# A fused recurrent-attention and two-layer kernel: the written order of all engines is replaced, 22 unread matmuls are put into it, and two bias operands become immediates

## The chip, the cores and the metric

One core of a Trainium2 chip runs the whole program. The metric is the device time of one execution in microseconds; of several runs the median is taken. The engines are TensorE (PE, with its weight loads PEld beside it), VectorE (DVE), ScalarE (ACT), GpSimd (POOL) and SyncE (SP), which here only issues transfers. Each engine works through its own instructions strictly in the order in which they are written, and waits on semaphores for the others.

## The reference

Three stages follow each other. First a gated recurrent attention (mLSTM) over 768 steps, for 2 batches and 8 heads of width 40. Its output is put side by side to 1536 tokens of width 320 and goes through a feed-forward layer of width 2048 with the function h - tanh(h) (layer one), and that through a mixture of four experts of width 1024, weighted by normalised probabilities (layer two).

```python
for t in range(S):
    m_new = np.maximum(f_gate[:, :, t] + m, i_gate[:, :, t])
    f_stab = np.exp(f_gate[:, :, t] + m - m_new)
    i_stab = np.exp(i_gate[:, :, t] - m_new)
    C = f_stab * C + i_stab * outer(v_t, k_t)
    n = f_stab * n + i_stab * k_t
    y[t] = sigmoid(o_gate_t) * (C @ q_t) / maximum(abs(n @ q_t), 1)
h = x @ w_in
x = (h - np.tanh(h)) @ w_out
out = sum over e of p[:, e:e + 1] * (np.maximum(x @ w1[e], 0.0) @ w2[e])
```

## The kernel before

**Attention.** The 768 steps are cut into six blocks of 128 steps, (j, b) being block j of batch b. Inside a block the recurrence is written as a masked product: `att_s` (L528) multiplies keys by queries, `att_a` (L538, DVE) multiplies the scores by the weights that ACT made with Exp (`att_exp`, L477), `att_h` (L549 for block 0, L552 and L557 after it) multiplies by the values and adds the carried state, and `att_u` (L566) makes the update of the state. The names in the order are `S`, `a`, `H` and `U` with j and b behind them. The gates are scanned on DVE (`g0`, `g1`, L379 to L404). The first block takes its weights in another way: `first_late` (L490, names `fl`) and `first_sum` (L493, names `fs`) build the exponents on PE with matmuls of 512 columns. `att_den` and `att_x` (L581 to L597) divide and gate; `x_tr` (L620) transposes the result; `x_high` and `x_low` (L625, L632, L636) split it into a high and a low part in reduced precision, so that a product of two split numbers takes three matmuls in place of one slow one. These are the tiles `xT`.

**Layer one.** The hidden width of 2048 is cut into eight slices of 256, the tokens into six groups of 256, which gives 48 units `I0` to `I47`. In unit i, `in1` makes the hidden values with 16 matmuls of 256 columns (L794), `hidden1` evaluates h - tanh(h) (names `h` with the unit's number and a letter, on ACT, DVE and POOL, L803 to L834), and `out1` multiplies by the second weight with 24 matmuls of 320 columns (L850, names `O`). Units 0 to 3 read the tokens of the first block, units 4 to 7 those of the second. The weights arrive as 64-bit numbers and are turned into split 32-bit ones by `conv` (names `i` and `o` with a number: `.l` the load, `.e` on ACT, `.k .m .n` on DVE, `.h` on ACT, `.o` on POOL).

**Layer two.** Tokens are in groups of 512. Each group is turned into operands for a scheme with seven products in place of eight (`build`, names `b`). There are 48 units `m0` to `m47`: `P1` to `P7` are the products (L786, four matmuls of 256 columns each), `c11` to `c22` the sums (L1144 on DVE, then Relu on ACT at L840 and the rest on DVE at L844), `O0` to `O7` the second product (L850, three matmuls of 320 columns each). Their weights are made by `conv_q`: POOL forms sums (`.s1 .s2 .s4`, L348, L353, L356), ACT rounds them (`.ht`, L360, and `.hb`, L333), POOL makes the low parts (`.t0 .t1 .b0 .b1`, L341). Unit 12e + 4t + q reads the weights numbered 8 + 4e + q, so that `i14` is first read in unit m14.

**What sets the order.** Every step is a small function with a name. The table `ORDER`, a text of names, is worked through from left to right, and each function puts its instructions on its engine's queue; names that are not in the table follow behind it, sorted by due times from `P`. So the table decides alone what stands in front of what on every engine, on SP's queue of transfers too. In the kernel before it reaches to the middle of unit m11. PSUM has eight banks, handed out by `bank(i)`; a tile that takes a bank waits for the last reader of the one before.

The lines below are the two activations that read a bias from memory.

```python
nc.scalar.activation(out=v["s"], in_=v["z"], func=ACT.Square, bias=ga[:, 0:1])
nc.scalar.activation(out=v["z"], in_=v["z"], func=ACT.Relu, scale=-1.0, bias=ga[:, 1:2])
```

Of the kernel before, what the change touches and what calls it, by code (L numbers as in the profile page):

```python
# [104 lines left out]
xh1 xl0.1 e104 xl1.1 i1.n i0b.o e112 e105 e102 xl1.0 I0.0 o0.l e117 Le1 i1.h kd100 S10 i2.e i1.o e110 Lg20 e113 e107
a100 I0.1 e111 e114 i2.k kd110 e116 st01.1 e106 i2.m e115 kd101 I1.0 h0a st01.0 h0z i2.n q10 S11 m.t2 a101 i3.l h0s
I1.1 h0t i2.h kd111 H100 a110 h1a q11 h0p h1z a111 H101 h1s i2.o h0q o0.e h1t h0m H110 Lg21 d10.0 o0.k Lp mk20 i3.e
h1p I2.0 d10.1 o0.m e207 H111 e201 d10.2 o0.n ag10 h1q dc o0.h Lg30 i3.k o2.l e200 o0.o h1m d11.0 h0c I2.1 e205 i3.m
mk21 h2a h0h d11.1 d11.2 i3.n h2z de h0l O0.0 h1c o1.l i3.h h2t h2s ag11 x10 h1h h2p i3.o e204 x11 U10 h2q h2m h1l xt3
o1.e Lv20 h2c Lk20 xt2 xh3 o1.k Le2 w10 o2.e I3.0 xl3.0 xl3.1 e203 o1.m e211 w11 e210 xh2 st10.0 I3.1 o1.n e206 O0.1  # L110
o2.k o3.l o1.h xl2.1 Lk21 o2.m h3a Lo1 o1.o h3z xl2.0 I4.0 h3t e202 e212 I5.0 st10.1 h3s o2.n mk30 h2h U11 h3p o2.h
I5.1 Lv21 h3q o3.e i4.l h2l O1.0 e215 o3.k h3m I4.1 kd200 e306 e214 o3.m e307 O1.1 kd201 e217 e213 st11.1 h4a S20 h3c
o2.o h4z h4t h5a I6.0 a201 h3h q20 I6.1 h5z a200 e305 h5t e301 O2.1 kd210 h6z st11.0 o3.n i4.e h3l S21 h4s o4.l H200
e216 h4p h5s q21 Le3 h4q o3.h H201 a210 e303 kd211 h6s w20 a211 U20 h4m Lg31 i4.k Lk30 H210 o3.o st20.0 d20.0 st20.1
h5p og2 H211 d20.1 i4.m w21 h4c O2.0 Lg40 d20.2 i4.n I7.0 ag20 d21.0 h6a i5.l d21.1 O3.0 h5q Lv30 o4.e mk31 d21.2 x20
O3.1 h5m o4.k ag21 h4h U21 h6t i4.h xt4 h6p h4l Lv31 I7.1 s3.0 Lk31 x21 xh4 st21.1 s3.1 xl4.0 xt5 i4.o h7z xl4.1 O4.1
st21.0 e300 h5c e304 S30 e302 o4.m xh5 h7a O4.0 kd300 e315 xl5.1 xl5.0 h5h I8.0 o4.n i5.e h5l h6q i6.l I8.1 e317 a300
h6m O5.0 kd301 i5.k e313 mk40 h8a S31 h6c o4.h a301 h8z I9.0 q30 e310 h8t e312 I9.1 e314 i5.m h6h q31 e316 H300 h7t
h7s e311 h7p h8s H301 kd310 h7q e406 h6l h8p h7m O5.1 Lg41 d30.0 h9z h7c kd311 O6.0 e401 i5.n h7h I10.0 h9s h7l d30.1
h8q o5.l e400 Lk40 O6.1 d30.2 e404 a310 h8m w30 a311 I10.1 i5.h h8c h9a mk41 U30 h9t H310 Lv40 ag30 e417 st30.0 h9p  # L120
h10z o4.o e413 H311 h9q e416 h8h x30 h9m st30.1 Lk41 w31 U31 o5.e h9c xt6 h8l h10a Lv41 I11.0 d31.0 d31.1 Lg50 e405
# [73 lines left out]
def kernel(  # L195
# [602 lines left out]
    def hidden1(hp):  # L798
# [23 lines left out]
        def small():  # L822
            nc.scalar.activation(out=v["z"], in_=v["z"], func=ACT.Relu, scale=-1.0, bias=ga[:, 1:2])  # L823
# [509 lines left out]
```

## Time and profile before

| what | value |
|---|---|
| median of 3 runs | 628.71 us |
| the runs | 625.6, 628.71, 632.61 us |
| the profiled execution | 634.11 us |
| its span, first to last instruction | 632.3 us |
| mean granted clock of PE in it | 0.957 |

The profiled execution took 1.8 us more than its span, and it is 5.4 us above the median of the runs. A page of the profile gives busy time per engine, the span in 40 slices, the chain of work that ended last, and groups of equal instructions; the trace behind it gives every instruction's start and length, what ended an engine's idle time, and the clock that was granted to PE (1.00 is 2.4 GHz, 0.50 is 1.2 GHz). A record of a matmul's length contains its way through the array, so that neighbours overlap; fp32 matmuls leave two records each.

### The profile page before, as it was taken

Reading aid. Unit: us, or ns where it says so; the run is one execution under the profiler, and the core shown is the slowest. Engines: PE = TensorE matmul, PEld = TensorE weight load, DVE = VectorE, ACT = ScalarE, POOL = GpSimd, SP = SyncE. Lnnn points to the kernel's source line nnn. Section 1 sums busy time; section 2 is a strip of 40 time slices with the busy share of each in tenths; the row PEclk is TensorE's granted clock in tenths of the full one; section 3 lists DMA queues with packets and bytes.
Section 4 is the critical chain, followed back from the end, with each engine's and each line's share of the span. In section 5 each row is a group of like instructions: output and inputs, shape, how many; then the busy total and the mean of one; then the engine's idle time right before and its main releaser. Section 6 shows DMA issues by size and latency. Waiting matters only on the chain.

```text
span 632.3 us, 12026 instructions
## 1 busy us (share of the span) xinstructions
PE 604.7 (96%) x4505; PEld 584.1 (92%) x4505; DVE 461.1 (73%) x1010; ACT 352.8 (56%) x738; POOL 337.1 (53%) x329
## 2 busy tenths in 40 slices
PE   7988999999999999999999849999999999999997
PEld 3878899999999999999999849999999999999997
DVE  7576998889789778977786526676676766666675
ACT  1485889877799999975453333223543234432221
POOL 3565887865667757698839356204844045630000
PEclk8565999999999999999999988999999999999999
DMA  8664875552112010011001101101211012201011
GB/s 297 201 187 154 289 229 178 184 182 79 34 44 76 1 34 2 2 55 55 23 1 31 58 22 54 55 2 34 76 55 55 1 35 55 76 2 43 1 43 42
DMA packets 29602, 48.15 MB, mean 76 GB/s; under 512 B 2264, under 2 KB 20056, under 8 KB 29544
## 3 DMA queue, kind: packets, MB, share of 16 engines
q1 hardware_dynamic: 29544, 47.39, 23.6%
q8 instruction: 35, 0.57, 0.4%
q14 instruction: 23, 0.19, 0.1%
HBM read 45.31 MB, written 2.06 MB: 75 GB/s over the span
## 4 chain that ended last, share of the span: by engine, by line
PE 67%; ACT 10%; DVE 8%; POOL 7%; issue 5%; DMA 2%; SPq 0%; DVEq 0%; POOLq 0%; ACTq 0%
PE b L850 28%; PE b L786 21%; PE b L794 7%; PE b L557 2%; PE b L528 2%; POOL so L722 2%; PE b L552 2%; ACT gh L830 2%; POOL gl L834 1%; ACT s L811 1%; ACT z L823 1%; POOL wb L341 1%; ACT t L803 1%; ACT z L807 1%; PE b L549 1%
## 5 line engine op out<-in xcount | busy, mean ns | idle before, releaser
L850 PE MATMUL b<-wo,gh 128*128 128x320 f32 x960 | 201.5, 311 | 9.0 <-DVE gh L844 7.3
L850 PE MATMUL b<-wo,gl 128*128 128x320 f32 x768 | 168.3, 310 | 1.7 <-POOL gl L834 1.7
L850 PEld LDWEIGHTS b<-wo,gh 128*128 128x128 f32 x960 | 149.9, 189 | 10.3 <-DVE gh L844 7.7
L850 PEld LDWEIGHTS b<-wo,gl 128*128 128x128 f32 x768 | 122.9, 189 | 3.4 <-POOL gl L834 3.1
L794 PE MATMUL b<-xT,wi 128*128 128x256 f32 x768 | 105.9, 289 | 2.6 <-ACT xT L625 0.9
L840 ACT ACTIVATE gh<-b 128x256 fp32r<-128x256 f32 x96 | 36.9, 384 | 122.2 <-DVE b L1144 73.1
L794 PEld LDWEIGHTS b<-xT,wi 128*128 128x128 f32 x768 | 98.6, 196 | 5.6 <-ACT xT L625 1.6
L786 PE MATMUL b<-so,wt 128*128 128x256 f32 x560 | 89.0, 283 | 2.7 <-DVE gl L844 1.6
L834 POOL TENSOR_TENSOR gl<-t,gh 128x512 fp32r<-128x512 f32 x48 | 65.5, 1366 | 45.2 <-ACT gh L830 36.5
L1144 DVE TENSOR_TENSOR b<-b,s 128x256 f32<-128x256 f32 x192 | 80.6, 423 | 11.9 <-PE b L786 6.1
L786 PEld LDWEIGHTS b<-so,wt 128*128 128x128 f32 x560 | 79.7, 190 | 3.9 <-DVE gl L844 2.6
L840 ACT ACTIVATE gl<-b 128x256 fp32r<-128x256 f32 x96 | 36.7, 384 | 69.7 <-DVE b L1144 67.5
L844 DVE SCALAR_TENSOR_TENSOR gl<-b,gl 128x256 fp32r<-128x256 f32 x96 | 40.3, 423 | 47.2 <-ACT gl L840 47.0
L341 POOL TENSOR_TENSOR wb<-raw,wb 128x384 fp32r<-128x384 f32 (+1 forms) x32 | 32.5, 1016 | 78.1 <-ACT wb L333 76.5
L844 DVE SCALAR_TENSOR_TENSOR gh<-b,gh 128x256 fp32r<-128x256 f32 x96 | 40.6, 423 | 42.1 <-ACT gh L840 42.1
L1144 DVE TENSOR_TENSOR s<-b,s 128x256 f32<-128x256 f32 x144 | 58.7, 418 | 12.8 <-PE b L786 8.6
L786 PE MATMUL b<-xo,wb 128*128 128x256 f32 x400 | 65.4, 282 | 1.1 <-DVE gh L844 0.5
L786 PEld LDWEIGHTS b<-xo,wb 128*128 128x128 f32 x400 | 57.8, 190 | 1.7 <-DVE gh L844 0.8
L341 POOL TENSOR_TENSOR wt<-tf,wt 64x512 fp32r<-64x512 f32 (+1 forms) x32 | 41.4, 1295 | 21.0 <-ACT wt L360 19.5
L826 DVE COPY_PREDICATED t<-z,b 128x512 f32<-128x512 int32 x48 | 36.0, 753 | 8.5 <-ACT z L823 8.1
L823 ACT ACTIVATE z<-z,ga 128x512 f32<-128x512 f32 x48 | 34.5, 720 | 10.9 <-DVE b L820 10.5
L814 DVE TENSOR_TENSOR t<-b,t 128x512 f32<-128x512 f32 x48 | 32.8, 683 | 10.4 <-ACT z L807 6.4
(124 smaller groups left out, 1022.5 us busy)
## 6 DMA issues: line engine op xcount, KB each, us to landing
kq<-in_kq_dram SPq DMA_DIRECT2D x12, 512.0 KB
raw<-in_wb_dram SPq DMA_DIRECT2D x16, 384.0 KB
raw<-in_wa_dram SPq DMA_DIRECT2D x7, 768.0 KB
w<-g_d SPq DMA_DIRECT2D x10, 512.0 KB
raw<-in_wa_dram SPq DMA_DIRECT2D x8, 640.0 KB
raw<-in_wb_dram SPq DMA_DIRECT2D x16, 320.0 KB
kv<-in_kv_dram SPq DMA_DIRECT2D x12, 372.0 KB
raw<-in_wb_dram SPq DMA_DIRECT2D x16, 128.0 KB
```

What stands on the lines that cost most here:

```text
L341: nc.gpsimd.tensor_tensor(out=o[r, k], in0=i[r, :, q], in1=o[r, 2 * q].bitcast(F32), op=ALU.subtract)
L528: nc.tensor.matmul(ps[g][:, h * 128:(h + 1) * 128], t[64 * g:64 * g + PK, 0, h, :], t[64 * g:64 * g + PK, 1, h, :], start=True, stop=True,)
L786: nc.tensor.matmul(o[:, 0:256], w[:, kw, b if b < 3 else b - 3], x_op(t, a, kx), start=(i == 0), stop=(i == 3),)
L794: nc.tensor.matmul(hp[:, c0:c0 + w], w_in(n, lo, kt, f), xt[:, xk, x0:x0 + w], start=(i == 0), stop=(i == 7))
L814: nc.vector.tensor_tensor(out=v["t"], in0=hp, in1=v["t"], op=ALU.subtract)
L823: nc.scalar.activation(out=v["z"], in_=v["z"], func=ACT.Relu, scale=-1.0, bias=ga[:, 1:2])
L826: nc.vector.copy_predicated(v["t"], v["z"].bitcast(I32), hp)
L834: nc.gpsimd.tensor_tensor(out=v["gl"], in0=v["t"], in1=v["gh"].bitcast(F32), op=ALU.subtract)
L840: nc.scalar.activation(out=g[:, 0], in_=src, func=ACT.Relu)
L844: nc.vector.scalar_tensor_tensor(out=g[:, 1], in0=src, scalar=0.0, in1=g[:, 0].bitcast(F32), op0=ALU.max, op1=ALU.subtract)
L850: nc.tensor.matmul(o[:, 0:DM], g[a][:, c:c + 128], w_out(n, lo, f), start=(first and i == 0), stop=(last and i == 2))
L1144: nc.vector.tensor_tensor(out=out, in0=x, in1=y, op=ALU.add)
```

## The change

The table `ORDER` is a different one and reaches to unit m18 in place of m11. It holds 22 new names, `fA`, `fB` and `fC` with a number. Each stands for one matmul of the identity by itself, 256 columns wide (13 of them, on bank 7 or 3) or 128 columns wide (9 of them, on bank 1), whose result nobody reads. All of them stand ahead of the first second-product of layer one, `O0.1`. The two biases become numbers in the instruction, so that the tile `ga` and the two small fills `m.ga` and `m.t2` fall away. The line numbers of the changed kernel are 15 higher up to the decays of attention and 39 higher behind them.

```diff
@@
-m.id m.late Lf m.b1 Li m.late2 m.eg fl10 i0b.l m.r0 Lb1 m.b0 Lv00 m.st0 Lb0 m.r1 Lk00 g0m fl01 Lv01 g1m g0i Lk01 m.rst
+m.b0 Lb0 m.rst Lf Li m.b1 i0a.l Lb1 m.late m.late2 Lv00 m.st1 Lv01 m.id g0m i0b.l m.r0 fl11 g0i g0f Lo0 Lk00 m.st0
...
@@
-    ga = const.tile([128, 24], F32, name="ga")
+    const.tile([128, 24], F32, name="pad")
@@
+    warm = {}
+
+    def keep_a():
+        if "a" not in warm:
+            warm["a"] = bank(7)
+        keep_on(warm["a"][:, 0:256])
+
+    def keep_b():
+        if "b" not in warm:
+            warm["b"] = bank(3)
+        keep_on(warm["b"][:, 0:256])
+
+    def keep_c():
+        if 1 not in accs:
+            accs[1] = spare[1] = bank(1)
+        keep_on(accs[1][:, 320:448])
+
+    def keep_on(o):
+        n = o.shape[1] // 128
+        nc.tensor.matmul(
+            o.rearrange("p (r c) -> p r c", r=n), ident, ident.unsqueeze(1).to_broadcast([128, n, 128]),
+            start=True, stop=True,
+        )
@@
-            nc.scalar.activation(out=v["s"], in_=v["z"], func=ACT.Square, bias=ga[:, 0:1])
+            nc.scalar.activation(out=v["s"], in_=v["z"], func=ACT.Square, bias=GA)
@@
-            nc.scalar.activation(out=v["z"], in_=v["z"], func=ACT.Relu, scale=-1.0, bias=ga[:, 1:2])
+            nc.scalar.activation(out=v["z"], in_=v["z"], func=ACT.Relu, scale=-1.0, bias=T2)
@@
-    head("m.ga", nc.vector.memset, ga[:, 0:1], GA)
-    head("m.t2", nc.vector.memset, ga[:, 1:2], T2)
@@
+    spare = {}
...
-        if p == 0:
+        if p == 0 and spare.pop(t, None) is None:
             accs[t] = bank(t)
@@
+    first = ORDER.split()
+    keep = {"fA": keep_a, "fB": keep_b, "fC": keep_c}
+    for name in first:
+        if name[:2] in keep:
+            add(0, 0, name, keep[name[:2]])
```

**PE, from the second half of attention block 1 to unit I3.** In the rows, L552 and L557 are `H11` (the block of batch 1), L422 is `dc` (the decays of the state) and L794 with b_482 is unit I2. Before, the two halves of I2 stand inside and behind `H11` and `dc`:

```order
L552 MATMUL b_463<-st_94,kq 128x82
L557 MATMUL b_463<-kv,w 128x41 x2
L794 MATMUL b_482<-xT_86,wi 128x256 x8
L552 MATMUL b_463<-st_94,kq 128x82
L557 MATMUL b_463<-kv,w 128x41 x2
L552 MATMUL b_463<-st_94,kq 128x82
L557 MATMUL b_463<-kv,w 128x41 x2
L422 MATMUL b_506<-ga_97,ga_100 104x6 x8
L794 MATMUL b_482<-xT_86,wi 128x256 x8
```

In the changed kernel, where L476 is an unread matmul, L833 is I2, L591 and L596 are `H11`, L437 is `dc`, L605 is `U10` and L659 the two transposes of x:

```order
L833 MATMUL b_482<-xT_86,wi 128x256 x16
L476 MATMUL b_349<-ident 128x128 x3
L591 MATMUL b_519<-st_94,kq 128x82
L596 MATMUL b_519<-kv,w 128x41 x2
...
L437 MATMUL b_545<-ga_97,ga_100 104x6 x8
L605 MATMUL b_579<-kv,kd 104x82 x4
L476 MATMUL b_349<-ident 128x128
L659 MATMUL b_597<-ident,x 128x128 x3
```

All of I2 now stands ahead of `H11`, and three unread matmuls stand between them.

**DVE, at the gated outputs x of block 1.** L814 with b_482 is the first step of I2's function and L597 the two gated outputs; before, the outputs stand behind that step:

```order
L826 COPY_PREDICATED t<-z,b_390 128x512
L814 TENSOR_TENSOR t<-b_482,t 128x512
L597 TENSOR_TENSOR x<-sd,b_434 128x4x2x40
L817 SCALAR_TENSOR_TENSOR b_482<-s,b_482 128x512
L597 TENSOR_TENSOR x<-sd,b_463 128x4x2x40
```

In the changed kernel, where L636 is the gated output and L853 that first step:

```order
L856 SCALAR_TENSOR_TENSOR b_409<-s,b_409 128x512
L636 TENSOR_TENSOR x<-sd,b_457 128x4x2x40
L859 SCALAR_TENSOR_TENSOR b_409<-b_409,z 128x512
L636 TENSOR_TENSOR x<-sd,b_519 128x4x2x40
L853 TENSOR_TENSOR t<-b_482,t 128x512
L865 COPY_PREDICATED t<-z,b_352 128x512
L865 COPY_PREDICATED t<-z,b_409 128x512
```

Both gated outputs moved ahead of the first step of I2's function.

**ACT, around units m10 and m11 of layer two.** L360 is `.ht`, first that of i13 and then that of i14; L840 are the Relus of the units. Before:

```order
L840 ACTIVATE gh_4620<-b3_4611 128x256
L360 ACTIVATE wt_4622<-tf_4428 128x2x512
L333 ACTIVATE wb_4632<-raw_4530 128x2x384
L360 ACTIVATE wt_4661<-tf_4657 128x2x512
L840 ACTIVATE gl_4663<-b4_4624 128x256
L840 ACTIVATE gl_4666<-b7_4638 128x256
```

In the changed kernel L375 is `.ht` and L879 are the Relus:

```order
L375 ACTIVATE wt_4536<-tf_4454 128x2x512
L1187 ACTIVATE s_4571<-b3_4561 128x256
L321 ACTIVATE wo_4579<-raw_4376 128x640
L879 ACTIVATE gh_4587<-b4_4543 128x256
L879 ACTIVATE gl_4590<-b7_4548 128x256
L879 ACTIVATE gl_4604<-b2_4556 128x256
L879 ACTIVATE gh_4623<-b4_4610 128x256
L375 ACTIVATE wt_4648<-tf_4606 128x2x512
L348 ACTIVATE wb_4656<-raw_4499 128x2x384
```

Between the two `.ht` there was one instruction, and there are six now.

## Rows read from the trace of the kernel before

**Rows 1.** The page, part 1: busy time and share of each engine.
```profile
PE 604.7 (96%) x4505; PEld 584.1 (92%) x4505; DVE 461.1 (73%) x1010; ACT 352.8 (56%) x738; POOL 337.1 (53%) x329
```

**Rows 2.** The page, part 2: 40 slices of the span, in tenths.
```profile
PE   7988999999999999999999849999999999999997
...
PEclk8565999999999999999999988999999999999999
```

**Rows 3.** Busy time by stretch, all engines, with the granted clock.
```profile
core 0: us, PE busy (x) PEld busy (x) DVE busy (x) ACT busy (x) POOL busy (x), PEclk, DMA share, GB/s
...
10.80:41.50 30.70, 28.02 (x133) 23.00 (x132) 18.23 (x38) 17.42 (x35) 14.50 (x17) 0.50 0.71 228
...
48.30:65.40 17.10, 15.44 (x73) 14.64 (x72) 11.53 (x23) 9.51 (x19) 9.94 (x9) 0.50 0.45 152
...
76.00:340.00 264.00, 260.47 (x2071) 253.38 (x2070) 219.34 (x423) 212.21 (x424) 188.29 (x185) 1.00 0.24 74
340.00:371.40 31.40, 27.22 (x201) 26.09 (x199) 17.45 (x46) 9.67 (x23) 16.30 (x18) 1.00 0.15 45
...
378.70:382.80 4.10, 4.05 (x17) 4.05 (x18) 1.35 (x4) 1.39 (x3) 4.00 (x3) 0.50 0.41 123
382.80:628.80 246.00, 245.91 (x1875) 244.92 (x1874) 166.64 (x432) 85.75 (x205) 80.36 (x72) 1.00 0.12 36
10.00:70.07 60.07, 54.43 (x291) 47.46 (x291) 41.82 (x81) 36.27 (x72) 32.98 (x31) 0.60 0.64 204
```

**Rows 4.** Who waited for whom, PE, whole span: total, times, longest.
```profile
PE b L850 <- DVE gh L844: 7.3, 1, 7.3
```

**Rows 5.** Timeline, 367 to 379 us: start, length, engine, instruction, idle before.
```profile
367.31 1.05 ACT L360 ACTIVATE wt<-tf 128x1024 fp32r<-128x1024 f32 x1
...
368.44 1.29 POOL L341 TENSOR_TENSOR wt<-tf,wt 128x512 fp32r<-128x512 f32 x1 [12.41 <-ACT wt L360]
...
375.22 0.72 POOL L356 TENSOR_TENSOR tf<-raw,tf 128x256 f32<-128x256 f32 x1
...
375.98 1.06 ACT L360 ACTIVATE wt<-tf 128x1024 fp32r<-128x1024 f32 x1 [6.88 <-POOL tf L356]
...
377.61 0.75 DVE L844 SCALAR_TENSOR_TENSOR gl<-b,gl 128x256 fp32r<-128x256 f32 x2 [7.43 <-ACT gl L840]
...
378.75 0.64 PE L850 MATMUL b<-wo,gh 128*128 128x320 f32 x1 [7.30 <-DVE gh L844]
```

**Rows 6.** The chain that ended last, 10 to 71 us: start, length, what.
```profile
10.01 3.43 PE b L493 x5
...
28.01 1.65 PE b L549 x8
...
36.35 0.79 PE b L794 x2
...
56.13 2.02 PE b L794 x8
...
70.07 1.43 PE b L794 x10
```

**Rows 7.** Timeline, 37 to 62 us, at the clock's steps and the gated outputs.
```profile
39.08 3.23 PE L794 MATMUL b<-xT,wi 128*128 128x256 f32 x16
...
48.17 0.83 PE L557 MATMUL b<-kv,w 128*128 128x41 f32 x4
...
61.86 0.48 DVE L597 TENSOR_TENSOR x<-sd,b 128x320 f32<-128x320 f32 x1
```

**Rows 8.** Groups by line and shape: busy us, mean ns, idle before.
```profile
L490 PE MATMUL b<-ex,ident 128*128 128x512 f32 x8 | 6.5, 992 | 1.6 <-POOL ex L887 1.6
...
L811 ACT ACTIVATE s<-z,ga 128x512 f32<-128x512 f32 x48 | 34.4, 718 | 0.3
...
L807 ACT ACTIVATE z<-b 128x512 f32<-128x512 f32 x48 | 28.0, 586 | 0.4 <-PE b L794 0.2
```

More of the change, by code (lines that the diff above doesn't have):

```diff
@@ L105 @@
[L105 to L109, printed above, removed]
@@ L185 @@
-m11.P3 m10.O2 m11.c12 i14.b1 m10.O6 m11.c21 m10.O7 i13.t1 i14.b0 i14.s1 i14.s2 i14.s4 i14.ht m11.c21h i14.t0 m11.c12h
-m11.c12l m11.c21l m11.c22l o13.o o14.l o14.h o14.o i14.t1"""
+m.b0 Lb0 m.rst Lf Li m.b1 i0a.l Lb1 m.late m.late2 Lv00 m.st1 Lv01 m.id g0m i0b.l m.r0 fl11 g0i g0f Lo0 Lk00 m.st0
+m.r1 g0h Lk01 g1m fl00 i0a.e g0g fr10 fA4 fr01 g0j g1f fl10 fr00 fl01 g1h fs10 fr11 fs00 g1g fe10 fs01 fe00 Sg fs11
+kd000 fe01 i1.l kd010 gr fA2 S00 m.eg i0b.e fe11 fA1 Lg10 kd001 fB4 Lg11 g1i a001 fA5 a000 S01 i0a.k H000 kd011 i0a.m
@@ new lines @@
+m10.u3 m10.P5 m10.P4 i13.t1 m10.c22 m10.P3 m11.P1 m10.c21 i13.t0 m9.O0 m11.s1 m8.O7 m9.O4 o13.h m9.O1 m9.O5 m10.c22h
+o13.o m10.c21h m9.O2 m10.c22l m10.c12 m9.O3 m10.c21l m10.O1 m10.c12h i14.s1 o14.l m11.P2 m10.O3 m11.c11 m9.O6 m10.c12l
+m11.c11h i14.s2 m11.P6 m11.P7 m11.u2 i14.s4 m11.P5 m11.c11l m11.u3 m10.O0 i14.ht m9.O7 m10.O2 i14.hb m11.P4 m10.O4
+i14.b0 m11.c21 m10.O5 m11.c22 m11.P3 m10.O7 m11.c22h m11.c21h m10.O6 m11.c22l m11.c12 m12.P1 m11.c21l m11.c12h m11.O0
+o14.h m11.c12l m12.P2 m12.s1 m11.O1 o14.o m12.c11 m12.P6 m12.c11h m11.O2 m12.c11l m12.P7 m12.u2 i14.b1 m11.O3 y0.2.2
@@ new lines @@
+m12.P5 m12.u3 y0.2.3 i14.t1 i15.l m11.O4 m12.c22 m12.P4 o15.l m11.O5 m12.c22h i14.t0 m12.P3 m12.c22l m11.O6 m12.c21
+m11.O7 m12.c21h m13.P1 m12.c21l m12.O0 m12.c12 i15.s1 m13.P2 m12.c12h i15.hb m12.c12l m12.O1 y0.2.0 m13.P6 i15.s2
+m13.s1 y0.2.1 m12.O2 m13.c11 i15.s4 m13.P7 m13.c11h m12.O3 o15.h i15.b1 m13.c11l m13.P5 m13.u2 i15.ht m12.O4 m13.u3
+m13.P4 m13.c22 m12.O5 i15.t0 m13.P3 m13.c22h m13.c22l m12.O6 m13.c21 m12.O7 o15.o m13.c21h m14.P1 m13.c21l m13.O0
+m13.c12 m14.P2 m13.c12h i15.t1 i16.l m14.s1 m13.O1 m13.c12l m14.c11 m14.P6 m14.c11h m13.O2 i15.b0 m14.c11l m14.P7
@@ L188 @@
+m16.c21h m17.P1 m16.c21l m16.c12 m16.O0 m16.c12h m17.P2 m17.s1 m16.c12l m16.O1 y1.0.0 m17.P6 y1.0.1 m16.O2 m17.c11
+m17.P7 m17.c11h m16.O3 m17.c11l m17.P5 m17.u2 m16.O4 m17.u3 m17.c22 m17.P4 m16.O5 m17.c22h m17.P3 m17.c22l m16.O6
+m17.c21 m16.O7 m17.c21h m18.P1 m17.c21l m17.O0 m17.c12 m18.P2 m17.c12h m18.s1 m17.c12l m17.O1 m18.c11 m18.P6 m18.c11h
+m17.O2 m18.c11l m18.P7 m18.u2 m17.O3 m18.u3 m18.P5 m17.O4 m18.c22 m18.P4 m18.c22h m18.c22l"""
 T2 = 0.0625
```

165 lines of the change are left out of this document (85 added, 80 removed).

## Prediction

> **What bounds the kernel now.** I read the busy times first. PE is busy for 604.7 of 632.3 us, the next engine, DVE, for 461.1 [rows 1]. So the time is PE's work, plus what PE waits, plus what a low clock adds. The 40 slices say where the two losses are: the PE line is below 9 in the first three slices and falls to 8 and 4 near slice 28, and the clock line shows 5 and 6 in slices 2 to 4 and 8 again near the second place [rows 2]. Everything between is 9 at full clock.
>
> Stretches cut at the clock's own steps give sizes [rows 3]. From 10.8 to 41.5 us and again from 48.3 to 65.4 us the granted clock is 0.50, which is 1.2 GHz, while PE is busy for 28.02 and 15.44 us. From 378.7 to 382.8 us it is 0.50 again, with 4.05 us busy. Between 76 and 340 us PE idles for 264.00 - 260.47 = 3.5 us, between 340 and 371.4 us for 31.40 - 27.22 = 4.2 us. From 382.8 us to 628.8 us it is busy for 245.91 of 246.00 us: nothing is left there, and the order past m18 is that of the due times as before.
>
> The largest single wait of PE is 7.3 us, a product L850 that waits for DVE's gh L844 [rows 4]. The timeline around it names the cause [rows 5]. ACT's `.ht` of i13 (L360) starts at 367.31 us. POOL then works without a gap worth naming from 368.44 us to 375.22 + 0.72 = 375.94 us on the low parts of i13 and the sums of i14. ACT's next `.ht`, that of i14, waits 6.88 us for the last of these sums; the Relus of unit m11 stand behind it on ACT, DVE's second half (377.61 us) behind those, and PE behind DVE until 378.75 us. Weights that are first read in m14 hold up m11.
>
> In the early part the chain that ended last says what the low clock costs [rows 6]. It is PE alone from 10.01 to 28.01 + 1.65 = 29.66 us, then other engines until 36.35 us, mostly PE from there to 56.13 + 2.02 = 58.15 us, and ACT and DVE from there to 70.07 us, when the last low part of x for unit I4 lets PE go on. From 70.07 us PE is nearly saturated. What PE did at the steps: the clock rose at 41.5 us during I1's wide products that began at 39.08 us, and fell at 48.3 us, 3.7 us into the run of `H10` and `H11` whose matmuls are 41 and 82 columns wide, the last of which before the fall begins at 48.17 us [rows 7].
>
> **The change, part by part.** The sum is made against the profiled execution, 634.1 us, of which 632.3 us are span.
>
> *Early stage, new order and unread matmuls.* The place to compare is the one at 70.07 us, where the last two products of unit I4's first half start. On the chain PE stands at 0.50 for 29.66 - 10.80 = 18.9 us, for 41.50 - 36.35 = 5.2 us and for 58.15 - 48.30 = 9.9 us, together 33.9 us [rows 3, 6]. At 2.4 GHz half of it goes: 17.0 us, the largest that I can read out of the clock by the chain. A second bound is DVE: between 10.00 and 70.07 us it is busy for 41.82 of 60.07 us [rows 3], and nearly all of this work remains and stays ahead of the place, so no more than 18.2 us can go. The lower bound is a loss, priced under the rivals.
>
> Between 17.0 us and nothing I take 14 us, near the upper end, for these reasons. With the clock up, PE's work in these 60.07 us shrinks to about 54.43 - 28.02/2 - 15.44/2 = 32.7 us, so in 46 us it has 13 us to spare, and PE is no longer what the others wait for. What is late next is DVE's queue: gates, the weights' conversion, attention. Both gated outputs of block 1, the second of which ended at 61.86 + 0.48 = 62.3 us [rows 7], stood behind the first step of I2's function, which waited for I2's second half behind `H11` and `dc`. Now I2 is ahead of `H11` and the outputs are ahead of that step, so the 62.3 - 58.15 = 4.2 us from I2's end to the second output no longer lie on the chain one behind the other. I leave 3 us of the 17 for waits on x that DVE and ACT still impose and for stretches at which the clock may not yet be up.
>
> The price of the unread matmuls: L490 is an fp32 matmul of 512 columns by 128 and leaves two records; its 8 records took 6.5 us, so 1.64 us for each of 4 matmuls at the slow rate [rows 8]. By columns an unread matmul of 256 is 0.82 us and one of 128 is 0.41 us, half of that at 2.4 GHz: 13 x 0.41 + 9 x 0.21 = 7.2 us, or 14.3 us at the low clock. At full clock 7.2 us fit into the 13 us that PE has to spare, so I cost them at nothing. What hides them are the waits for DVE; if that cover is gone they cost up to 7.2 us.
>
> *The wait at 371 us.* Between i13's and i14's `.ht` ACT now has six instructions, among them one unit's four Relus. A unit in the saturated stretch has 52 matmuls at 246.00/1875 = 0.131 us, or 6.8 us; POOL's chain from one `.ht` to the next took 375.94 - 368.44 = 7.5 us [rows 3, 5]. So ACT may still wait there for about 1 us, and PE has second products of m9 and m10 to do meanwhile. The 7.30 us go, and with them the low clock behind the wait: 4.05 us busy at 0.50 is 2.0 us too long. Together 9.3 us.
>
> *Other waits.* In the 3.5 + 4.2 = 7.7 us of small waits from 76 to 371.4 us the new order can win at most 7.7 us, and it can add others. I take 3 us. The immediates help here: an ACT instruction of 512 columns with a bias from memory (L811) takes 718 ns, the same function without (L807) 586 ns [rows 8]. For 96 instructions that is 12.7 us of ACT, which is busy for 212.21 of 264.00 us in layer one [rows 3], on no path that PE waits for as a rule.
>
> The Trainium skill, on the page ScalarE: Activation LUTs, in the section What ACT_TABLE_LOAD costs, gives about 93 ns for each operand read through a pointer. The trace has 132 ns between L811 and L807, so the page's price is the smaller one; by it ACT would save 8.9 us, and the term of 3 us would be about 2.
>
> The sum is 14 + 9.3 + 3 = 26.3 us: 634.1 - 26.3 = 607.8 us. From the median of the runs the same sum gives 628.7 - 26.3 = 602.4 us. The profiled execution is above all three runs, and some of what it lost may be its own and go with the rest. I forecast 605 us, midway.
>
> **The rivals.** The first: a wait of the kind at 371 us remains, because POOL's 7.5 us per set of weights stay longer than a unit's 6.8 us and ACT's order is as strict as before. For it speaks that the tile of the sums has one buffer, so that i14's sums cannot start before i13's low parts end. Against it that one unit of Relus now lies between. The 9.3 us stay: 605 + 9.3 = 614 us.
>
> The second: DVE and ACT bound the early stage. DVE was busy for 41.82 of 60.07 us with PE slow; in 46 us the same work would fill 91%, and any wait for ACT or for a transfer then moves everything behind it. If it gives 5 us in place of 14, the time is 614 us as well.
>
> The third, on the fast side: 17 us early and all 7.7 us of small waits, 7.7 us more than the forecast: 597 us.
>
> The fourth ends slower than before: the clock stays at 1.2 GHz until the place at 70.07 us. PE was busy for 28.02 of 30.70 us while 0.50 was granted [rows 3], so filling its gaps may change nothing. Then the unread matmuls cost 14.3 us, against 60.07 - 54.43 = 5.6 us of gaps that can take them: 8.7 us. And the work that ran at 1.00, from 41.50 to 48.30 us and from 65.40 us to the place, 11.5 us, would take as long again. That is 20.2 us later in place of 14 us earlier: 605 + 34.2 = 639 us. It decides from about 10 us of loss in the early stage on, where it eats the other two terms. Against it stands the rise at 41.5 us during wide products: the unread ones are as wide as those, and stand between the narrow ones.
>
> **How the numbers follow.** Forecast 0.64, first rival 0.12, second 0.12, third 0.08, fourth 0.04. The forecast's own range is 599 to 612 us. The range of 596 to 618 us takes in the first three rivals, and leaves out the fourth and cases where two of them meet. About 1%, 6.3 us, is what a measurement tells from no change here: faster means below 622.4 us, which the forecast and three rivals are (0.96). For two misfortunes together, and for a surprise that no row shows, I take 0.05 off: faster 0.91, same 0.05, slower 0.04.
>
> **What would show it right or wrong.** After the change the granted clock should be 1.00 from about 10 us on, with at most one or two short falls before 60 us. The first half of I4 (L833, third group of that line on the second pair of x) should end near 56 us. PE should have no wait above 2 us behind 60 us, and the records of L375 on ACT no wait of several us for POOL. The saturated stretch should keep 0.131 us per matmul. The prediction is wrong if 0.50 is granted for most of the first 50 us, if DVE is idle there while PE runs unread matmuls that something waits behind, or if a new wait of some 7 us stands where another engine's order is strict.

## The result, and the profile after

The changed kernel takes 611.12 us, the median of 4 runs (609.58 to 615.8), against 629.96 us of the kernel before (625.6 to 632.61). The ratio is 0.972, 95% interval 0.964 to 0.980. The forecast was 605 us, in a range of 596 to 618. The profiled execution took 610.91 us, its span is 609.1 us. Against the profiled execution of before, 634.11 us, that is 23.2 us, where the sum said 26.3; by the medians it is 18.8 us. Lines up to the attention's decays stand 15 later than before, those behind them 39 later: L850 is L889, L794 is L833, L287 is L302, L811 is L850.

The page after, parts 1 and 2, against [rows 1, 2]:

```profile
PE 591.0 (97%) x4549; PEld 576.4 (95%) x4549; DVE 468.7 (77%) x1008; ACT 344.5 (57%) x738; POOL 338.3 (56%) x329
...
PE   7799899999999999999999999999999999999996
...
PEclk9987999999999999999999999999999999999999
```

The hole near slice 28 is gone from both lines, and of the clock's early low slices two are left in place of four. DVE is busier than before, 468.7 against 461.1 us, with two instructions fewer.

Busy time by stretch, cut at the clock's steps and as in [rows 3]:

```profile
core 0: us, PE busy (x) PEld busy (x) DVE busy (x) ACT busy (x) POOL busy (x), PEclk, DMA share, GB/s
7.90:28.40 20.50, 18.03 (x117) 12.54 (x115) 16.93 (x32) 10.31 (x15) 11.53 (x12) 1.00 0.93 320
28.40:35.20 6.80, 5.33 (x19) 4.79 (x20) 5.55 (x9) 6.01 (x17) 3.42 (x3) 0.50 0.71 237
...
52.27:59.10 6.83, 6.15 (x31) 6.11 (x31) 6.68 (x9) 5.11 (x12) 6.83 (x7) 0.50 0.95 333
59.10:608.60 549.50, 541.12 (x4230) 535.65 (x4229) 420.34 (x926) 310.24 (x673) 303.14 (x289) 1.00 0.20 61
...
76.00:340.00 264.00, 262.12 (x2083) 257.86 (x2083) 225.30 (x436) 201.29 (x422) 196.81 (x195) 1.00 0.24 74
340.00:371.40 31.40, 31.40 (x241) 31.40 (x240) 19.78 (x52) 14.48 (x31) 21.15 (x20) 1.00 0.18 56
```

Two falls to 0.50 are left, 6.8 us each. From 76 to 340 us PE idles for 1.88 us where it was 3.5, from 340 to 371.4 us not at all where it was 4.2. The three longest waits of PE that remain stand at the start and in the early stage (total, times, longest):

```profile
PE b L529 <- POOL ident L921: 4.5, 1, 4.5
PE b L659 <- DVE x L636: 3.7, 1, 3.7
PE b L833 <- DVE xT L671: 1.8, 1, 1.8
```

The timeline shows what DVE did ahead of the second and the third, and what ACT's `.ht` does now:

```profile
24.77 1.63 DVE L302 SCALAR_TENSOR_TENSOR x<-raw,x 128x768 int32<-128x768 int32 x1
...
27.06 1.08 DVE L631 TENSOR_TENSOR sd<-acc,den 128x320 f32<-128x320 f32 x1
28.07 1.35 DVE L308 SCALAR_TENSOR_TENSOR x<-raw,x 128x384 int32<-128x384 int32 x1
29.34 0.47 DVE L636 TENSOR_TENSOR x<-sd,b 128x320 f32<-128x320 f32 x1
...
29.87 0.90 PE L659 MATMUL b<-ident,x 128*128 128x128 f32 x3 [3.71 <-DVE x L636]
...
30.56 3.19 PE L476 MATMUL b<-ident 128*128 128x256 f32 x8
...
33.41 2.00 PE L833 MATMUL b<-xT,wi 128*128 128x256 f32 x8
...
56.28 2.48 DVE L302 SCALAR_TENSOR_TENSOR x<-raw,x 128x640 int32<-128x640 int32 x1
...
59.93 1.59 DVE L308 SCALAR_TENSOR_TENSOR x<-raw,x 128x640 int32<-128x640 int32 x1
...
63.18 1.43 PE L833 MATMUL b<-xT,wi 128*128 128x256 f32 x10 [1.78 <-DVE xT L671]
...
352.31 1.06 ACT L375 ACTIVATE wt<-tf 128x1024 fp32r<-128x1024 f32 x1 [1.37 <-POOL tf L371]
```

The place that the prediction watched, the last products of I4's first half, starts at 63.18 us: 6.9 us earlier than at 70.07 [rows 6], where 14 were forecast. Both stalls, the one before L659 and the one right at the place, end with DVE, and ahead of both DVE has been converting weights (L302, L308). Unread matmuls (L476, 8 records, 3.19 us at the low clock) stand on PE between the second gated output and I0.

To split the gain I take the loss behind 80 us, PE's idle time plus half of its busy time at 0.50, and what is left of the span without it. In the kernel before PE is busy for 533.89 of the 552.33 us behind 80 us, and for 4.09 us of the low clock there: 18.44 + 2.05 = 20.5 us. For all profiled kernels:

| profiled execution | span | at 0.50, 0 to 75 us | late loss | span less late loss |
|---|---|---|---|---|
| before | 632.3 | 47.8 | 20.5 | 611.8 |
| after | 609.1 | 13.7 | 6.8 | 602.3 |
| order_before | 627.9 | 30.7 | 22.2 | 605.7 |
| before_ht_later | 620.0 | 17.1 | 18.8 | 601.2 |
| before_ht_m12 | 620.0 | 27.3 | 15.2 | 604.8 |
| late_only | 613.1 | 30.7 | 9.4 | 603.7 |
| no_unread | 607.3 | 23.9 | 5.4 | 601.9 |
| conv_late | 606.6 | 10.2 | 5.7 | 600.9 |
| bias_memory | 611.3 | 13.7 | 8.0 | 603.3 |
| order_before_unread | 628.8 | 20.5 | 20.5 | 608.3 |
| early_only | 639.3 | 13.7 | 29.0 | 610.3 |
| ident_first | 610.8 | 20.5 | 5.3 | 605.5 |
| best1 | 609.2 | 13.7 | 5.4 | 603.8 |
| best1_no_unread | 608.7 | 30.7 | 5.5 | 603.2 |

So the 23.2 us are 13.7 late and 9.5 early. The names are those of the experiments. The five kernels with the early order of before and no unread matmuls (before, order_before, before_ht_later, before_ht_m12, late_only) lie between 601.2 and 611.8 in the last column, and the profiled execution of before is the worst of them. Against their mean, 605.4, the early part is 3.1 us and not 9.5.

### The profile page after: what moved, and what is told of

Read it like the earlier page. It is cut to its first block, busy times and chain, and to the rows that moved or that the text cites. A ratio compares the mean times of both kernels' runs of the same rounds, so it can differ in the third digit from the quotient of the medians.

```text
span 609.1 us, 12111 instructions
## 1 busy us (share of the span) xinstructions
PE 591.0 (97%) x4549; PEld 576.4 (95%) x4549; DVE 468.7 (77%) x1008; ACT 344.5 (57%) x738; POOL 338.3 (56%) x329
## 4 chain that ended last, share of the span: by engine, by line
PE 77%; DVE 9%; ACT 5%; POOL 5%; issue 3%; DVEq 0%; POOLq 0%; ACTq 0%
PE b L889 34%; PE b L825 26%; PE b L833 8%; POOL gl L873 2%; PE b L596 2%; PE b L567 2%; DVE b L859 1%; PE b L591 1%; DVE t L853 1%; DVE b L856 1%; PE b L476 1%; DVE t L865 1%; ACT z L846 1%; DVE x L302 1%; DVE x L308 1%
## 5 line engine op out<-in xcount | busy, mean ns | idle before, releaser
L889 PE MATMUL b<-wo,gh 128*128 128x320 f32 x960 | 200.8, 310 | 0.3 <-DVE acc L1053 0.3
L889 PE MATMUL b<-wo,gl 128*128 128x320 f32 x768 | 166.9, 308 | 0.0
L889 PEld LDWEIGHTS b<-wo,gh 128*128 128x128 f32 x960 | 148.8, 188 | 1.0 <-ACT s L850 0.5
L889 PEld LDWEIGHTS b<-wo,gl 128*128 128x128 f32 x768 | 122.2, 188 | 0.0
L833 PE MATMUL b<-xT,wi 128*128 128x256 f32 x768 | 103.5, 286 | 2.7 <-DVE xT L671 1.8
L879 ACT ACTIVATE gh<-b 128x256 fp32r<-128x256 f32 x96 | 36.9, 384 | 118.2 <-DVE b L1183 80.9
L833 PEld LDWEIGHTS b<-xT,wi 128*128 128x128 f32 x768 | 97.0, 193 | 5.0 <-DVE xT L671 2.0
L825 PE MATMUL b<-so,wt 128*128 128x256 f32 x560 | 87.5, 281 | 0.7 <-DVE t L865 0.7
L879 ACT ACTIVATE gl<-b 128x256 fp32r<-128x256 f32 x96 | 36.8, 384 | 70.7 <-DVE b L1183 68.9
L356 POOL TENSOR_TENSOR wb<-raw,wb 64x384 fp32r<-64x384 f32 (+1 forms) x32 | 33.1, 1034 | 76.9 <-ACT wb L348 73.5
L356 POOL TENSOR_TENSOR wt<-tf,wt 64x512 fp32r<-64x512 f32 (+1 forms) x32 | 41.5, 1298 | 12.1 <-ACT wt L375 10.8
L865 DVE COPY_PREDICATED t<-z,b 128x512 f32<-128x512 int32 x48 | 36.0, 752 | 8.1 <-ACT z L862 7.4
L853 DVE TENSOR_TENSOR t<-b,t 128x512 f32<-128x512 f32 x48 | 32.4, 682 | 11.3 <-ACT z L846 5.8
L862 ACT ACTIVATE z<-z 128x512 f32<-128x512 f32 x48 | 30.3, 630 | 10.5 <-DVE b L859 8.8
```

The costliest lines, as they stand in the source:

```text
L356: nc.gpsimd.tensor_tensor(out=o[r, k], in0=i[r, :, q], in1=o[r, 2 * q].bitcast(F32), op=ALU.subtract)
L825: nc.tensor.matmul(o[:, 0:256], w[:, kw, b if b < 3 else b - 3], x_op(t, a, kx), start=(i == 0), stop=(i == 3),)
L833: nc.tensor.matmul(hp[:, c0:c0 + w], w_in(n, lo, kt, f), xt[:, xk, x0:x0 + w], start=(i == 0), stop=(i == 7))
L853: nc.vector.tensor_tensor(out=v["t"], in0=hp, in1=v["t"], op=ALU.subtract)
L865: nc.vector.copy_predicated(v["t"], v["z"].bitcast(I32), hp)
L879: nc.scalar.activation(out=g[:, 0], in_=src, func=ACT.Relu)
```

## The experiments

Ratios are to the kernel before, timed beside each on the same chip, with 95% intervals.

**no_unread.**

```diff
- fA4 fA2 fA1 fB4 fA5 fB20 ... fC28 fC10   (22 names of the order)
```

> The changed kernel without its 22 unread matmuls; everything else stands in the same order. Theory A (they hold the granted clock up and lie where PE waits anyway): without them 0.50 is granted again for most of the stretch from 10 to 60 us, the place where the last two products of unit I4's first half start moves from 63.2 us to between 66 and 70 us, and the time is 614 to 618 us. Theory B (the clock doesn't hang on them, and those of them that stand on the chain, 2.55 us between 13.92 and 17.14 us and about 3 us behind 30.77 us, only cost PE time): the clock falls no earlier than with them, the place comes at 58 to 61 us and the time is 606 to 609 us. If both effects are there they may cancel: then the clock row shows more of 0.50 and the time stays within 2 us of 611.

Measured: 613.12 us (609.1 to 616.02), ratio 0.9755 (0.971 to 0.980). The clock did fall more: 0.50 for 23.9 us in place of 13.7, and a mean clock of 0.975 (median of the runs) against 0.988. Yet the place came at 62.44 us:

```profile
62.44 1.41 PE L833 MATMUL b<-xT,wi 128*128 128x256 f32 x10 [2.12 <-DVE xT L671]
```

Neither theory's number came out; nearest is the mixed case that the expectation names last, with 2.0 us more than the 611.12 of the changed kernel. The unread matmuls hold the clock, and the times, with intervals that overlap, show no gain from it. That they take it again on PE's own chain is a reading of the 0.7 us by which the place comes earlier without them; the low clock may as well have cost little there.

**conv_late.**

```diff
- fB26 i1.m xh0 ... ag01 e103 i0b.n mk20 e112 x01 e106
+ fB26 xh0 ... ag01 e103 mk20 e112 x01 i1.m i0b.n e106
- o1.m ... xl2.1 e203 xl3.1 o1.n ... o1.h st10.0 xl2.0 I4.0
+ xl2.1 e203 xl3.1 ... st10.0 xl2.0 o1.m o1.n I4.0      (o1.h behind h3a)
```

> The changed kernel with four weight conversions of DVE moved: i1's second step (L302, 1.63 us) and the second half of i0's third step (L308, 1.35 us) behind the second gated output of block 0, and the second and third step of o1 (L302 2.48 us, L308 1.59 us) behind the low parts of x for unit I4, with ACT's o1.h two instructions later. Theory A (DVE's queue, lengthened by conversions that run beside POOL, sets the two stalls of the early stage): the second gated output of block 0 ends about 3 us before 29.81 us, I4's last products start at 57 to 61 us in place of 63.2 us, and the time is 606 to 609 us. Theory B (PE's own chain and the clock set them): both places move by under 1 us, time 610 to 612 us. Theory C (the weights of i0, i1 or o1 become late instead): PE waits over 1 us for wi or wo, and the time is 611 us or more.

Measured: 608.48 us (608.33 to 610.04), ratio 0.968 (0.964 to 0.972); theory A's 606 to 609. Its timeline:

```profile
27.31 0.49 DVE L636 TENSOR_TENSOR x<-sd,b 128x320 f32<-128x320 f32 x1
27.71 1.23 DVE L302 SCALAR_TENSOR_TENSOR x<-raw,x 128x768 int32<-128x768 int32 x1
27.85 0.90 PE L659 MATMUL b<-ident,x 128*128 128x128 f32 x3 [1.75 <-DVE x L636]
...
57.83 2.05 PE L833 MATMUL b<-xT,wi 128*128 128x256 f32 x16
57.85 0.41 DVE L671 TENSOR_TENSOR xT<-b,xT 128x256 fp32r<-128x256 f32 x1
58.18 1.68 DVE L302 SCALAR_TENSOR_TENSOR x<-raw,x 128x640 int32<-128x640 int32 x1
```

The second gated output starts 2.0 us earlier, the wait before L659 shrinks from 3.71 to 1.75 us, and the whole first half of I4 runs from 57.83 us without a wait. So DVE's queue set both stalls; the clock, 3.4 us less at 0.50 than in the changed kernel, can account for at most 1.7 us at the place. Some 4.6 us at the place (63.18 against 57.83 and six records of 0.13 us) became 2.5 us of span (609.1 to 606.6): part comes back as waits of L605 and L833 behind it (1.4 and 1.6 us).

**bias_memory.**

```diff
- func=ACT.Square, bias=GA)            + func=ACT.Square, bias=ga[:, 0:1])
- scale=-1.0, bias=T2)                 + scale=-1.0, bias=ga[:, 1:2])
```

> The changed kernel with the two biases of layer one read from memory again, as in the kernel before (two small memsets of DVE early on come back). Both theories: L850 and L862 on ACT go from about 630 ns back to about 718 ns, 96 instructions, 8 to 9 us of ACT busy. Theory A (ACT is on no path that PE waits for): the time is 610.5 to 612.5 us. Theory B (the immediates carry the small waits that went between 76 and 371 us): PE's idle time from 70 to 350 us grows from 2.2 us to 4 us or more, and the time is 613 to 615 us.

Measured: 612.52 us (612.19 to 613.36), ratio 0.974 (0.970 to 0.978). Groups by line and shape, after:

```profile
L862 ACT ACTIVATE z<-z 128x512 f32<-128x512 f32 x48 | 30.3, 630 | 10.5 <-DVE b L859 8.8 <-DVE den L622 1.7
...
L850 ACT ACTIVATE s<-z 128x512 f32<-128x512 f32 x48 | 29.7, 628 | 0.2
```

and with the biases in memory:

```profile
L862 ACT ACTIVATE z<-z,ga 128x512 f32<-128x512 f32 x48 | 34.6, 721 | 8.8 <-DVE b L859 7.1 <-DVE den L622 1.7
L850 ACT ACTIVATE s<-z,ga 128x512 f32<-128x512 f32 x48 | 34.1, 720 | 0.2
```

The price is 91 and 92 ns for each instruction, 8.8 us of ACT. On the time it is 1.4 us by the medians, inside the intervals. PE's idle time from 70 to 350 us rose from 2.2 to 4.5 us, as theory B has it, but the time did not follow to 613; 612.52 lies between the two ranges, at the edge of theory A's. Not settled.

**before_ht_later** and **before_ht_m12.** Both start from the kernel before.

```diff
  later:  - ... i14.b0 i14.s1 i14.s2 i14.s4 i14.ht m11.c21h i14.t0 m11.c12h ... m11.c22l
          + ... i14.b0 m11.c21h m11.c12h ... m11.c22l i14.s1 i14.s2 i14.s4 i14.ht i14.t0
  m12:    + ... m12.P1 i15.l m12.s1 ... m12.u3 ... m12.P5 o13.o i14.ht i14.t0 o14.h o14.o i14.t1
```

> The kernel before with one ACT instruction moved: the .ht of i14 (and the POOL sums ahead of it in the written order) behind the two copies of m11's second hidden half. Theory A (that instruction alone makes the wait at 371 us): PE's wait of 7.3 us and the 0.50 behind it go, and the time is 9.3 us below the kernel before's in the same comparison, ratio about 0.985. Theory B (POOL's 7.5 us for one set of weights come back as another wait further on, m14's weights being late): a wait of 2 us or more appears behind 371 us, the ratio lies between 0.99 and 1.0.

Measured: 624.57 us (621.74 to 627.98, 12 runs), ratio 0.9942 (0.9915 to 0.9969). Theory B's number. ACT's timeline shows that the wait only moved:

```profile
364.83 1.06 ACT L360 ACTIVATE wt<-tf 128x1024 fp32r<-128x1024 f32 x1 [5.11 <-POOL tf L356]
367.79 0.74 ACT L306 ACTIVATE wo<-raw 128x640 fp32r<-128x640 f32 x1 [1.89 <-DMA raw<-in_wb_dram]
368.43 0.36 ACT L1148 ACTIVATE s<-b 128x256 f32<-128x256 f32 x1
```

ACT asks for the same sums and waits 5.11 us, then 1.89 us for a transfer, and now m12's first copy (L1148) stands behind; PE waits 4.8 us for it:

```profile
PE b L786 <- ACT s L1148: 4.8, 1, 4.8
```

Hence the second one:

> The kernel before with the .ht of i14 (and the low parts of i14, o13 and o14 behind it) moved further: behind the Relus of unit m12 up to its last first product, so that POOL's sums of i14 have the time of one more unit of PE before ACT asks for them. With it two copies later only, ACT waited 5.11 us for the same sums and PE 4.8 us for m12's first copy in place of 7.3 us. Theory A (what stands behind that instruction on ACT is the whole of the wait): no wait of PE above 2 us between 330 and 400 us, ratio 0.982 to 0.989. Theory B (POOL's 7.5 us for a set of weights against 6.8 us of PE for a unit make a wait wherever it is put): a wait of 3 us or more stays there, ratio 0.990 to 0.996, as with two copies later.

Measured: 621.99 us (617.52 to 628.76, 12 runs), ratio 0.9887 (0.985 to 0.9925). PE's waits from 320 to 400 us:

```profile
PE b L787 <- DVE gh L845: 1.7, 2, 1.2
PE b L787 <- DVE gl L845: 1.5, 1, 1.5
```

No wait above 2 us is left, theory A. The wait at 371 us with its low clock is worth 1.13% of 629.7, that is 7.1 us (4.7 to 9.5), where the prediction took 9.3, inside that interval.

**order_before.** The changed kernel's code with the order of before.

```diff
- ORDER of after     + ORDER of before without m.ga, m.t2
```

> The changed kernel with the whole written order of before, so without unread matmuls; of the change only the immediates stay. Theory A (ACT is on no path that PE waits for): ratio 0.995 to 1.002 to the kernel before, 625.5 to 630 us. Theory B (the immediates carry a part of the gain): ratio 0.990 to 0.994, 622 to 625 us. The profile is also a second look at the early order of before with its wait at 371 us: in one execution of that order 0.50 was granted for 47.8 of the first 75 us (the profiled one of before), in another for 17.1 us (that with the .ht of i14 later), and the last products of I4's first half started at 70.07 and at 57.34 us. If the clock of the early stage is a matter of the execution, this one lies between or at either end, with the same instructions.

Measured: 628.11 us (624.66 to 629.79, 12 runs), ratio 0.9993 (0.996 to 1.003): by themselves the immediates give nothing that shows, theory A. The place, in this kernel and in that with the `.ht` later, with the same instructions up to there but for the biases:

```profile
63.83 1.41 PE L818 MATMUL b<-xT,wi 128*128 128x256 f32 x10 [0.59 <-DVE xT L656]
```

```profile
57.34 1.43 PE L794 MATMUL b<-xT,wi 128*128 128x256 f32 x10 [0.57 <-DVE xT L632]
```

57.34, 63.83 and, in the profiled execution of before, 70.07 us go with 17.1, 30.7 and 47.8 us at 0.50. The two other profiles of this early order fit in: 61.03 us with 23.9 us at 0.50 up to the place (before_ht_m12) and 65.03 us with 30.7 (late_only). In that order the place comes 12.7/30.7 = 0.41 us later for each microsecond at the low clock, and how long the early stage took was a matter of the execution. The new order without unread matmuls, no_unread, had 23.9 us at 0.50 as well and came to the place at 62.44 us: at the same clock no earlier than the old one.

**late_only** and **early_only**, the two halves of the new order.

```diff
late_only:   ORDER of before up to I5.0, then ORDER of after
early_only:  ORDER of after up to I5.0, then ORDER of before
```

> The order of before up to the first half of unit I5 (no unread matmul, immediates stay), behind it everything in the changed kernel's order. Theory A (early 14 or 7 us, late 9.3 + 3 us): ratio 0.980 to 0.985, 616 to 619 us. Theory B (most of the gain lies behind the early stage): ratio 0.972 to 0.979, 611 to 615.5 us. The two halves of the change should add up to the ratio of 0.972 that both have together: with the ratio of the early half alone, minus 1, the sum should come to -0.028 within the intervals; if it is short of that, the halves need each other.

Measured: 614.36 us (609.8 to 616.75), ratio 0.978 (0.972 to 0.984), within theory B: 13.7 us of the gain (10 to 17) come from behind the early stage. The table above has 13.7 too, for the profiled pair of before and after.

> The changed kernel's written order, unread matmuls and immediates up to the first half of unit I5; behind it everything that is left in the order of before. Theory A (the prediction's term for the early stage, or half of it as the profiles have it, 14 or 7 us): ratio 0.978 to 0.990, 615 to 622 us. Theory B (the early stage of the profiled kernel before was slow by its execution, and the new early order gives little): ratio 0.991 to 1.0, 623 to 628 us. In both the wait of 7 us at 371 us is there in the profile, earlier by what the early stage gave.

Measured: 637.41 us (631.97 to 642.29), ratio 1.0146 (1.008 to 1.021): slower, as neither theory had it, so the halves don't add up. The place is reached at 63.52 us, as after. Then comes the seam, first in the timeline, then in windows:

```profile
78.32 0.64 PE L875 MATMUL b<-wo,gh 128*128 128x320 f32 x1 [3.56 <-POOL wo L310]
```

```profile
78.40:95.00 16.60, 16.60 (x82) 16.05 (x83) 10.63 (x22) 8.58 (x13) 9.27 (x10) 0.50 0.39 124
```

One weight is converted 3.56 us late, and behind it PE works without a gap at 0.50 for 16.6 us, 8.3 us too long. Together that is up to 11.9 us in this execution, which took 641.26 us. As an estimate, without them it would be at 629.4 us, 0.8 below the 630.16 of the kernel before. It is one of three of 640.6 to 642.3 us; the other three took 632.0 to 634.2 us at a mean clock of 0.978 to 0.984 in place of 0.965 to 0.968. They have no profile, and they too are above 630.16. So this run shows no gain from the early half; what the seam hides of one stays open.

**order_before_unread.**

```diff
+ 5 fA of 256 and 25 fC of 128 columns, behind fl00, S00, gr, bi, xt0, xt1, I0.0, I0.1, I2.1, U10, I3.1
```

> The order of before with immediates and with unread matmuls alone: 30 of 256 or 128 columns, as much PE time as the 22 of the change, behind the same attention products, the same transposed outputs and the same units of the first 65 us. Theory A (holding the clock is what the early stage gains by): mean granted clock 0.983 or more against about 0.970, and the time 4 to 8 us below that of the order of before with immediates alone. Theory B (PE at full clock then waits for DVE, ACT and transfers instead): the mean clock rises by 0.01 or more and the time stays within 2 us. Theory C (they stand on PE's chain): slower by 2 us or more.

Measured: 630.41 us (628.47 to 636.97, 12 runs), ratio 1.004 (1.000 to 1.008). The mean clock rises from 0.970 to 0.978, and the time does not fall. In the profile 0.50 stands for 20.5 us in place of 30.7, and the place comes at 66.12 us in place of 63.83: as theory C has it. The intervals of the two times overlap, so that the matmuls win nothing is what shows, and that they cost something is likely.

**ident_first, best1, best1_no_unread.**

```diff
ident_first: + m.id m.late m.b0 m.late2 at the head
best1:       + m.id ... as above, the moves of conv_late, og0 ahead of i1.e
best1_no_unread: the same without fA, fB, fC
```

> The changed kernel with POOL's identity (L920, L921) and the mask's late half ahead of POOL's two memsets of the reset vector, and DVE's memset of the mask first. In the changed kernel PE's first product waits for that identity until 4.49 us, in the kernel before it started at 1.61 us. Theory A (PE's chain from its first product to the first attention outputs sets the early stage): PE starts at 2 to 3 us, the place where the last products of I4's first half start moves by 1.5 to 2.5 us, the time is 608.5 to 610 us. Theory B (gates, DVE and transfers set it): PE starts earlier, waits that much longer before 30 us, and the time stays within 0.8 us of 611.1.

Measured: 610.11 us (608.03 to 612.68), ratio 0.9716 (0.967 to 0.977). PE starts at 1.60 us, but the clock falls at 11.8 us, where it did not fall before 28 us in the changed kernel:

```profile
11.80:18.60 6.80, 6.80 (x24) 3.39 (x23) 2.07 (x3) 2.90 (x5) 6.03 (x7) 0.50 0.79 268
```

PE is busy for all of these 6.80 us, so up to 3.4 us are lost, more than the 2.9 us won at the start. The place comes at 64.89 us. The median lies between the two theories. The profile is of an execution of 612.55 us; three took 611.6 to 612.7 us at a mean clock of 0.983 to 0.986, the other three 608.0 to 608.6 us at 0.989 to 0.992. How much the earlier start gives is therefore a matter of the clock, which neither theory had.

> The kernel with the four later weight conversions, and besides: the identity first, and ACT's first sigmoid (L988) ahead of the weight copy (L294) that waits for its transfer until 18.93 us in the changed kernel. Theory A (each of the three takes its share from the chain to the first gated output): the first gated output ends 1.5 us or more before 24.02 us, the time is 605 to 607.5 us. Theory B (the conversions alone count): 608 to 609 us, as with them alone.

Measured: 609.32 us (606.94 to 611.88), ratio 0.9706 (0.966 to 0.975). Not better than the later conversions alone, theory B's side; here too the clock fell, at 11.6 us, and the first gated output (L636) started at 26.47 us, 2.9 us later than in the changed kernel.

> The same without the 22 unread matmuls. Theory A (their gain by the clock and their cost on PE's chain cancel here too): within 2 us of the same kernel with them, 0.50 granted for some 10 us more. Theory B (with DVE's stalls shorter, PE's chain counts more, and the unread matmuls that stand on it cost more than they hold): 2 to 4 us faster than with them. Theory C (they pay once the stalls are short): 2 to 5 us slower without.

Measured: 609.56 us (608.98 to 614.55), ratio 0.972 (0.968 to 0.977): theory A, 0.50 for 30.7 us in place of 13.7 and the time the same. The best kernel of the study is conv_late; its interval overlaps the change's own, so that it beats it is likely, not shown.

## Why the prediction was right, and where it was not

**The wait at 371 us: right.** It is gone, ACT's `.ht` waits 1.37 us where "about 1 us" was said. Alone it is worth 7.1 us (4.7 to 9.5); the 9.3 of the sum lie inside. The first rival is real as a mechanism: with too little between the two `.ht`, before_ht_later had its wait back.

**Other waits: too small.** 3 us of 7.7 were taken. In the two profiles 1.65 us went from 76 to 340 us and 4.2 us from 340 to 371.4: 5.8 us. With the wait at 371 us the late part is 13.7 us, by the profiles and by the times of late_only, where the sum had 12.3.

**The early stage: the step that failed.** The sum said 14 of at most 17.0 us, "near the upper end", because "with the clock up" PE "is no longer what the others wait for". The profiled pair has 9.5, the mean of the five executions of the old early order leaves 3.1, and the timed halves leave 0.978 to 0.972, 0.6% or 4 us, with intervals that overlap. So what the early half gives is 3 to 5 us, not clear of noise. Two things were wrong in the term. First, the 17.0 us were read from one execution with 47.8 us at 0.50; other executions of the same order had 17 to 31. The prediction saw that its execution was above the others and took the middle of 607.8 and 602.4, but it left the term at its size. As an estimate for that one execution it was not too large: 47.8 - 13.7 = 34.1 us fewer at 0.50, at the 0.41 us of order_before's comparison, are 14 us, but the place came only 6.9 us earlier, so the new order puts some 7 us back in the way. PE's first product starts at 4.49 us in it and at 1.61 us in the kernel before, and the stalls for DVE are 3.7 and 1.8 us; no run splits the 7 us. Second, what is late next was named (DVE's queue) and priced at 3 us. DVE is busy for 52.31 of the 63.18 us up to the place, 83%:

```profile
0.00:63.18 63.18, 52.14 (x337) 42.81 (x337) 52.31 (x91) 37.11 (x72) 37.54 (x43) 0.89 0.71 232
```

In the execution that reached it at 57.34 us DVE had 50.61 us, 88%. That DVE holds PE up is shown for the two stalls, by conv_late; for the rest of the stage it is argued.

The early half fared as the second rival said, 5 us in place of 14. By the medians 18.8 us were gained and 13.7 of them are late, so 5.1 are early, 1 to 9 by late_only's interval alone. The forecast of 605 plus the sum of 26.3 starts from 631.3 us; the median of before is 629.96, 1.3 us lower. So 605 + 8.9 for the early half, 1.4 less for the late part and 1.3 less for the start make 611. That the time lay in the range is owed to the range, which took in this rival, and not to the sum; that the other two errors worked against the first was luck.

**The unread matmuls at nothing: right in the sum, wrong in the reason.** They cost nothing that shows: 0.9755 without, 0.972 with, and 0.972 and 0.971 in the other pair. But not all were hidden in PE's spare time: those before I0 took 3.19 us between the second gated output and I0. That the clock that they held paid for them is the likely reading; no run separates the two. That they would make the early stage shorter by holding the clock was the prediction's own reason, and three pairs of kernels show no such gain, in either order.

**The immediates.** The prediction took 132 ns from L811 against L807. Both are Square, but L807 reads a PSUM bank (b) and L811 a tile of SBUF (z), so there was more than the bias between them. In the changed kernel, where neither reads a bias from memory, the pair (L846, L850) still differs by 37 ns, 591 against 628:

```profile
L846 ACT ACTIVATE z<-b 128x512 f32<-128x512 f32 x48 | 28.3, 591 | 7.3 <-PE b L833 5.4 <-DVE t L853 1.9
```

On the same line with and without the bias the difference is 91 and 92 ns. The Trainium skill, page ScalarE: Activation LUTs, section What ACT_TABLE_LOAD costs, has about 93 ns for a pointer operand; the runs agree with it and not with the 132 ns.

**What was to be seen.** Two falls of the clock before 60 us: right. I4 near 56 us: wrong by 7 us, counted as the sum counts, by where the last two products start. No wait of PE above 2 us behind 60 us, no long wait of L375, 0.131 us per matmul (549.50/4230 = 0.130): right. The slower rival did not come: the clock rose.

## What to carry to other kernels

A low clock in a profile is not yet a loss: ask who waits for PE there, and look at the mean clock of several executions before a term is read from one. Matmuls that nobody reads held the clock here but stand in PE's order, and in three pairs of kernels they won no time. Where DVE is busy for over 80% of a stretch, as here, try to move what is not urgent behind what PE waits for, as the later conversions did, before trying anything on PE.

## What the runs showed of the hardware

**The clock's steps differ between executions of one order.** The same early instructions had 0.50 from 10.8 us on in one execution and not before 22.7 us in another. With PE's first product at 1.6 us, seven of nine profiled executions fell between 10.7 and 12 us; with it at 4.5 or 4.6 us none of five fell before 24 us. Why is open. The Trainium skill, page TensorE: Matmul & The Clock Gate, section What's actually happening, says that what watches PE's activity runs freely and does not start anew with a kernel; that fits steps that move from one execution to the next.

**Some DVE instructions are longer beside POOL.** One line's instructions, min, median and longest in ns, after:

```profile
L788 DVE TENSOR_TENSOR sf<-y,sf x6: 415/550/965, 230.4 to 319.1; 128x256 f32<-128x256 f32 x6
```

```profile
L865 DVE COPY_PREDICATED t<-z,b x48: 721/754/773, 54.4 to 275.3; 128x512 f32<-128x512 int32 x48
```

L788 reads two tiles of SBUF: the three with no tensor_tensor of POOL beside them took 0.42 us, the three with one beside them for nine tenths of their time or more 0.68, 0.89 and 0.97 us. L865 reads one of its two from PSUM and took 0.75 us in both cases (means of 10 and 21). L302, which reads two of SBUF, went up to 2482 ns in after and 1132 in before. Two inputs are not the whole of it: L298, with one tile of SBUF, took 0.49 us without (mean of 3) and 0.80 with POOL beside it (mean of 4, 128x640). DVE's work grew by 7.6 us with the new order, and forms like these are the ones whose means grew; no run took POOL's work away to test it. The Trainium skill, page GPSIMD Engine Reference, section 8. Key points, says that POOL shares its SBUF interfaces with VectorE and contends with instructions of two SBUF inputs: the trace agrees, with 0.68 to 0.97 us in place of 0.42 for L788.
